# Five filling matmuls of 512 columns become 45 of 32 columns in a hash-attention and MLP kernel on one core

## The chip, the core and the metric

The kernel runs on one core of a Trainium2 chip. A core has five engines with instruction streams of their own: TensorE (matrix multiply; its records are PE for matmuls and PEld for weight loads), VectorE (DVE), ScalarE (ACT), GpSimd (POOL) and SyncE (SP), which here only issues transfers. They work side by side and wait for each other by semaphores. Operands lie in an on-chip memory of 128 partitions (SBUF), matmuls write to accumulators (PSUM), and the DMA engines move data between these and the device's memory.

The metric is the device time of one execution in microseconds. Before the change it is 292.64 us, the median of three runs (292.36 to 292.85).

## What is computed

Attention over 4 batches, 8 heads, 768 positions and 64 dimensions, in which a query sees only the keys of its own bucket; a bucket is given by the signs of six projections. Then a normalised two-layer MLP with a residual, on rows of 512 features.

```python
q_bits = (np.einsum('bhsd,dk->bhsk', q, proj) > 0).astype(np.int64)
k_bits = (np.einsum('bhsd,dk->bhsk', k, proj) > 0).astype(np.int64)
...
mask = q_bucket[:, :, :, None] == k_bucket[:, :, None, :]
scores = scale * np.matmul(q, k.transpose(0, 1, 3, 2))
scores = np.where(mask, scores, -1000000000.0)
...
return np.matmul(attn, v).astype(np.float32)
...
xn = (x - mu) / np.sqrt(var + 1e-06) * g_ln
ch = np.maximum(xn @ w_ch1, 0.0) @ w_ch2
return (x + ch).astype(np.float32)
```

## The kernel before

The work is cut into twelve units `u` of 256 query rows (three to a batch). Each unit runs through six score steps `s`, for two groups of four heads and three stretches of 256 keys, and then through the MLP.

- `S_` (matmuls of line 570) makes the scores of one step in three passes: one multiplies the sign bits `G`, which puts queries and keys of different buckets far apart, and two multiply q and k (`qb`, `kb`). Each pass runs as four matmuls on 32 rows of the array. `E_` (line 576) is the exponential on ScalarE. `A_` (line 595) multiplies its result with the values: 16 matmuls of 65 columns to a step, each with weights of its own, so 48 matmuls where three steps follow each other.
- `na`, `nb`, `nc_`, `ag` and `ce` (lines 608 to 630) normalise on VectorE. `F_` (line 659) and `P_` (line 726) are the two MLP layers on TensorE; the first unit's second layer is `D_` (line 674). `R_`, `Y_` and `ss` between them run on VectorE and ScalarE.
- The first batch's inputs are prepared on the fly at the start: `lx` loads q and k, `tn` transposes them on VectorE (line 304), `ca` casts them, `ha` or `hc` project them (lines 394 and 405), `sl` spreads the bits (line 418), `bh`, `bc` and `bi` turn them into `G`. `ft` (line 644) and `fc` (line 652) transpose the first unit's rows; the result is `xnT`.
- The weights of the MLP are loaded by eight transfers of 512 KB that GpSimd issues (`lw1`, `lw2`, lines 446 and 457) on the software queue q0; the other loads, the masks and the outputs go through the hardware queue q1, issued by SyncE.

No scheduler decides the order: the string `ORDER` lists every step as `name.engine.arguments`, each engine takes its own steps in that order, and semaphores are put in where one needs another's result. So TensorE's instructions form one fixed stream, and instructions are fetched from memory while the kernel runs, on DMA queues of their own that the profile calls "instruction".

TensorE's stream begins with fillers, matmuls of ones whose results nobody reads. `warm` issues eight of 512 columns while the first loads are under way. After it `wm` issues one more of 512 columns each time it stands in the order: `wm.t.0` and `wm.t.1` directly behind `warm`, `wm.t.2` and `wm.t.3` behind the first projections of step 0, ahead of its scores, and `wm.t.6` ahead of the scores of step 2:

```python
lg.s on.p.0 mem.v tab.a pf.v warm.t wm.t.0 wm.t.1 sel.p tn.v.0.0.0
p32.p tn.v.0.1.0 on.p.1 ca.a.0.0.0 pmem.p ha.t.0.0.0 bh.v.0.0.0 ha.t.0.1.0 bh.v.0.1.0 wm.t.2
wm.t.3 ca.a.0.1.0 tn.v.0.1.1 ca.p.0.1.1 tn.v.0.1.2 S.t.0.2 E.a.0.0 E.a.0.1 ha.t.0.1.1 bh.v.0.1.1
ha.t.0.1.2 bh.v.0.1.2 wm.t.6 ...
```

A weight load belongs to every matmul; in the profile each is a record of its own. `ones` is 128 x 128, and `row(4, P)` reads it four times, which gives the 512 columns.

Of the kernel before, what the change touches and what calls it, by code (L numbers as in the profile page):

```python
# [159 lines left out]
    x="012301320132",  # L160
# [5 lines left out]
def kernel(  # L166
# [15 lines left out]
    nc = tc.nc  # L182
    P = 128
# [35 lines left out]
    ones = pool.tile([P, P], BF16, name="ones")  # L219
# [9 lines left out]
    made, taken = {}, {}  # L229
# [127 lines left out]
    def row(n, m):  # L357
        return ones[:, :m].unsqueeze(1).to_broadcast([P, n, m])
# [4 lines left out]
            nc.tensor.matmul(wp[:, 0].rearrange("p (a x) -> p a x", x=P), ones, row(4, P), start=True, stop=True)  # L363

    def wm(eng, n):
        nc.tensor.matmul(
            made["warm"][:, 0].rearrange("p (a x) -> p a x", x=P), ones, row(4, P), start=True, stop=True,
        )

    def lx(eng, g, t, kp0, kp1):  # L370
        src = qk_view(t, 0, g).rearrange("p (c kp x) -> p c kp x", c=CC, kp=3)
# [364 lines left out]
    def O_(eng, u, *a):  # L736
# [11 lines left out]

    OPS = dict(
        mem=mem, pmem=pmem, tab=tab, lp=lp, sel=sel, pf=pf, p32=p32c, warm=warm, wm=wm, lx=lx, tn=tn, ca=ca, ha=ha, bh=bh, hc=hc, bc=bc, sl=sl, bi=bi, lg=lg, gt=gt, gc=gc,  # L750
        lw1=lw1, wg=wg, lw2=lw2, on=on, lv=lv, cv=cv, su=su, sp=sp, sq=sq, sc=scp, LX=LX, gx=gx, tu=tu, CA=CA, hm=hm, bt=bt, mw=mw, mr=mr,
        S=S_, E=E_, A=A_, wa=wa, na=na, nb=nb, nc=nc_, ag=ag, ce=ce, rs=rs, fl=fl, ft=ft, fc=fc, F=F_, R=R_, D=D_, Z=Z_, P=P_, Y=Y_, sw=sw, ss=ss, O=O_,
# [37 lines left out]
```

## Time and profile before

| | |
|---|---|
| time, median of three runs | 292.64 us |
| the profiled execution | 292.61 us, span of its instructions 290.9 us |
| TensorE's matmuls | 4645, weight loads 4647 |
| `wm` (line 366) | 5 matmuls, first start 4.3 us, last 9.9 us |
| `warm` (line 363) | 8 matmuls, 1.1 to 4.1 us |
| DMA, mean over the span | 117 GB/s, 34.10 MB |

The profile is of one execution. Times in it count from the start of the span. A timeline row gives the start, the duration, the engine, the line and the operation (output and inputs by the program's names, the shapes, and how many it stands for); in brackets stands the idle time of the engine ahead of it and what ended it. "issue" means that the profile shows nothing that the engine waited for. A row of a table by windows gives the window, its length, then for each engine the busy time and, as "x", the number of records in it, then TensorE's granted clock, the mean busy share of the DMA engines, and the GB/s moved. In the DMA view a row gives a queue, its packets, MB, and the time that they took as a share of 16 engines over the window; shares can add up to more than 100%, since an engine can have two packets under way.

### The profile page before, as it was taken

The numbers are of one execution on the slowest core, as the hardware profiler recorded it, in microseconds if no ns is written. First come the engines' busy times: TensorE is split into PE (matmuls) and PEld (weight loads), VectorE is DVE, ScalarE is ACT, GpSimd is POOL, SyncE is SP. The second block draws the span as 40 slices with busy tenths as digits, with TensorE's granted clock in tenths as the row PEclk, the third lists the DMA queues.
The fourth block names the chain that finished last, engine by engine and source line by source line (L and its number), as shares of the span: only waits on it lengthen the run. The fifth ranks groups of instructions, "written<-read, shape, count | busy, mean of one in ns | idle before, by whom it ended". The sixth has DMA issues, their size and how long they took to land.

```text
span 290.9 us, 10520 instructions
## 1 busy us (share of the span) xinstructions
PE 282.9 (97%) x4645; PEld 227.0 (78%) x4647; DVE 207.0 (71%) x478; ACT 206.7 (71%) x236; POOL 53.8 (18%) x88
## 2 busy tenths in 40 slices
PE   8998999999999999999999999999999999999994
PEld 4776777648788887888778878877888878898883
DVE  5758898896779795797667995876665655782653
ACT  4889998998966978784865996887794694515140
POOL 4560426232431005000300107210010010001000
PEclk9999999999999999999999999999999999999999
DMA  6999997646544591364430352220310301404022
GB/s 191 365 303 271 214 278 135 141 116 167 179 122 130 132 335 56 125 114 136 95 82 1 83 133 64 61 55 7 92 34 8 74 2 24 107 0 99 12 74 73
DMA packets 31055, 34.10 MB, mean 117 GB/s; under 512 B 15521, under 2 KB 27809, under 8 KB 31010
## 3 DMA queue, kind: packets, MB, share of 16 engines
q1 hardware_dynamic: 25938, 28.72, 35.3%
q0 software_dynamic: 4224, 4.19, 8.7%
q8 instruction: 36, 0.59, 0.9%
q10 hardware_dynamic: 848, 0.53, 0.7%
q14 instruction: 9, 0.07, 0.1%
HBM read 27.86 MB, written 6.88 MB: 119 GB/s over the span
## 4 chain that ended last, share of the span: by engine, by line
PE 95%; DVE 2%; ACT 1%; issue 1%; ACTq 0%; DVEq 0%
PE f L659 30%; PE sc L570 18%; PE X L726 13%; PE acc L595 13%; PE Yb L726 7%; PE Ya L726 3%; PE hp L526 3%; PE hf L394 3%; PE f L674 2%; PE warm L363 1%; ACT E L576 1%; DVE xnT L652 0%; PE hf L405 0%; PE vp L487 0%; PE Yc L726 0%
## 5 line engine op out<-in xcount | busy, mean ns | idle before, releaser
L576 ACT ACTIVATE E<-sc,bias_sb 128x1024 bf16<-128x1024 f32 x144 | 153.2, 1112 | 34.3 <-PE sc L570 31.1
L659 PE MATMUL f<-xnT,w_sb 128*128 128x256 bf16 x768 | 94.2, 273 | 0.2 <-DVE xnT L652 0.2
L659 PEld LDWEIGHTS <-w_sb 128*128 128x128 bf16 x768 | 71.5, 98 | 12.6 <-issue 5.0
L667 ACT ACTIVATE hb<-f 128x512 bf16<-128x512 f32 x67 | 39.7, 598 | 34.1 <-PE f L659 34.1
L570 PE MATMUL sc<-qb,kb 32*128 32x256 bf16 x1152 | 52.4, 267 | 0.0
L595 PE MATMUL acc<-vaug,E 128*128 128x65 bf16 x1152 | 43.9, 194 | 0.9 <-issue 0.9
L595 PEld LDWEIGHTS <-E 128*128 128x128 bf16 x1152 | 40.9, 98 | 5.0 <-issue 3.7
L570 PE MATMUL sc<-G 6*128 6x256 bf16 (+1 forms) x576 | 42.3, 273 | 0.9 <-ACT E L576 0.8
L726 PEld LDWEIGHTS <-hb 128*128 128x128 bf16 x352 | 33.4, 98 | 5.4 <-issue 1.3
L635 POOL TENSOR_SCALAR rs<-mv 128x2 f32<-128x2 f32 x12 | 3.3, 278 | 152.5 <-DVE mv L624 152.4
L570 PEld LDWEIGHTS <-kb 32*128 32x128 bf16 x1152 | 30.3, 93 | 1.5
L731 DVE TENSOR_TENSOR x<-X,x 128x256 f32<-128x256 f32 x44 | 18.4, 420 | 15.6 <-PE X L726 15.3
L570 PEld LDWEIGHTS <-G 6*128 6x128 bf16 (+1 forms) x576 | 15.8, 91 | 16.3 <-issue 13.5
L669 DVE TENSOR_SCALAR hb<-f 128x512 bf16<-128x512 f32 x29 | 19.8, 682 | 12.2 <-PE f L659 12.0
L726 PEld LDWEIGHTS <-S 128*128 128x128 bf16 x264 | 25.0, 98 | 4.5 <-issue 1.3
L304 DVE STREAM_TRANSPOSE T<-X 128x384 f32<-128x384 f32 (+2 forms) x52 | 26.1, 536 | 0.0
L608 DVE SCALAR_TENSOR_TENSOR y<-vsB,acc 128x520 f32<-128x520 f32 x24 | 16.6, 692 | 9.8 <-PE acc L595 9.5
L726 PE MATMUL Yb<-w_sb,S 128*128 128x256 bf16 x176 | 22.9, 273 | 0.0
L726 PE MATMUL X<-wt,hb 128*128 128x256 bf16 x168 | 21.8, 273 | 0.0
L621 DVE BATCH_NORM_STATS2 st<-x 128x6 f32<-128x256 f32 x48 | 17.4, 412 | 0.2
L617 DVE TENSOR_TENSOR x<-y,rc 128x512 f32<-128x512 f32 x24 | 16.6, 692 | 0.8
L731 DVE TENSOR_TENSOR x<-Yb,x 128x256 f32<-128x256 f32 x22 | 9.3, 421 | 9.7 <-PE Yb L726 9.5
(95 smaller groups left out, 266.4 us busy)
## 6 DMA issues: line engine op xcount, KB each, us to landing
out_dram<-x SPq DMA_DIRECT2D x45, 128.0 KB
X<-in_k_dram SPq DMA_DIRECT2D x7, 768.0 KB
vn<-in_v_dram SPq DMA_DIRECT2D x24, 192.0 KB
X<-in_q_dram SPq DMA_DIRECT2D x6, 768.0 KB
w_sb<-in_moe_w_ch_dram POOLq DMA_DIRECT2D x8, 512.0 KB, 11.7
vn<-in_v_dram SPq DMA_DIRECT2D x2, 768.0 KB
X<-in_q_dram SPq DMA_DIRECT2D x2, 512.0 KB
Bd<-B SPq DMA_DIRECT2D x6, 96.0 KB
```

The lines of the kernel that those rows point to most:

```text
L304: nc.vector.transpose(d[:, j], s[:, j, kj0 : kj0 + n])
L570: nc.tensor.matmul(sc(s, i // 2)[:, i % 2, 256 * kk : 256 * kk + 256], lh, rh, start=(rep == 0), stop=(rep == 2), skip_group_check=True,)
L576: nc.scalar.activation(E(s)[:, heads(h)], sc(s, h), AF.Exp, scale=EXP_SCALE, bias=bias_sb)
L595: nc.tensor.matmul(acc[:, qt, (D + 1) * i : (D + 1) * (i + 1)], E(s)[:, i, 256 * kk + P * qt : 256 * kk + P * qt + P], vaug(u // 3)[:, 4 * ...
L608: nc.vector.scalar_tensor_tensor(yt(u, g), vs, EPS_ROW, made[f"acc{u}{g}"][:, :, :A], op0=AOP.mult, op1=AOP.add,)
L617: nc.vector.tensor_tensor(xo, a[:, :, :, 0:D], rc.to_broadcast([P, 2, 4, D]), op=AOP.mult)
L621: nc.vector.bn_stats(stats(u)[:, qt, g], xt(u)[:, qt, 256 * g : 256 * g + 256])
L659: nc.tensor.matmul(f1[:, n].rearrange("p (t x) -> p t x", t=2), w1_sb[:, dt, P * nt : P * nt + P], xnT(u)[:, :, dt], start=(dt == 0), stop ...
L667: nc.scalar.activation(hb(u)[:, 2 * p : 2 * p + 2], f1, AF.Relu)
L669: eng.tensor_scalar_max(hb(u)[:, 2 * p : 2 * p + 2], f1, 0.0)
L726: nc.tensor.matmul(f2, lh[:, n], rh[:, n], start=(first and n == 0), stop=(n == 7), skip_group_check=True)
L731: nc.vector.tensor_tensor(x, made[f"{prod(u, k)}{u}"], x, op=AOP.add)
```

## The change

`wm` issues a number of matmuls in place of one: 6 for `wm.t.0` and `wm.t.1`, 11 for `wm.t.2`, `wm.t.3` and `wm.t.6`, 45 in all. Each multiplies `ones` by the first 32 columns of `ones` and writes to the first 32 columns of the same accumulator. Forty more matmuls and forty more weight loads stand in TensorE's stream ahead of the scores of step 2. The order string is the same, and so are the streams of the other engines and the waits.

```diff
     def wm(eng, n):
-        nc.tensor.matmul(
-            made["warm"][:, 0].rearrange("p (a x) -> p a x", x=P), ones, row(4, P), start=True, stop=True,
-        )
+        for _ in range(6 if n < 2 else 11):
+            nc.tensor.matmul(made["warm"][:, 0, :32], ones, ones[:, :32], start=True, stop=True)
```

## The prediction

> **What bounds the kernel now.** I read the page first, then TensorE's waits, then the stretches around the two breaks that they show, and last the DMA view cut into short windows.
>
> ```profile
> span 290.9 us, 10520 instructions
> PE 282.9 (97%) x4645; PEld 227.0 (78%) x4647; DVE 207.0 (71%) x478; ACT 206.7 (71%) x236; POOL 53.8 (18%) x88
> q8 instruction: 36, 0.59, 0.9%
> PE 95%; DVE 2%; ACT 1%; issue 1%; ACTq 0%; DVEq 0%
> ...
> PE acc L595 <- issue: 0.9, 2, 0.6
> ```
>
> TensorE sets the end: it is busy for 97% of the span and makes 95% of the chain that ended last. So the time is the sum of its work and of its breaks. The last row, from the view of its waits, counts two breaks at line 595 that are put down to "issue", that is, to nothing that the profile shows. The timeline shows both (start, duration, idle time before it in brackets):
>
> ```profile
> 23.97 1.43 PE L595 MATMUL acc<-vaug,E 128*128 128x65 bf16 x41
> 25.74 0.27 PEld L595 LDWEIGHTS <-E 128*128 128x128 bf16 x7 [0.48 <-issue]
> ...
> 41.91 0.29 PE L418 MATMUL hf<-Bc,spread 128*128 128x64 bf16 x4
> 42.03 1.26 PE L595 MATMUL acc<-vaug,E 128*128 128x65 bf16 x36
> 43.86 0.42 PEld L595 LDWEIGHTS <-E 128*128 128x128 bf16 x12 [0.68 <-issue]
> ```
>
> Each break cuts a run of 48 equal matmuls in two (41 + 7, 36 + 12), where no other engine is waited for. Together they cost 0.48 + 0.68 = 1.16 us. The distance between them says what they are:
>
> ```profile
> 25.73:43.85 18.12, 16.62 (x383) 13.11 (x383) 16.07 (x39) 16.94 (x22) 4.95 (x9) 1.00 1.10 243
> ```
>
> From one break to the other TensorE runs 383 matmuls and 383 weight loads, 766 records. Queue q8 of the page fetches instructions in 36 packets, 0.59 MB; TensorE's 4645 + 4647 = 9292 records make 258 a packet, so a packet is 16 KB and holds some 256 instructions. 766 is three packets: both breaks stand at the edge of a block of instructions. Counted from them, five successive old blocks start and end here (window, its length, then TensorE's busy time and counts):
>
> ```profile
> 19.91:25.73 5.82, 5.00 (x133) 3.81 (x131) 3.92 (x11) 5.75 (x7) 0.83 (x2) 1.00 1.09 321
> 25.73:33.09 7.36, 6.41 (x127) 5.32 (x128) 6.67 (x17) 6.91 (x9) 1.10 (x3) 1.00 1.07 192
> 33.09:38.67 5.58, 5.58 (x129) 4.34 (x130) 4.56 (x11) 5.33 (x8) 3.62 (x6) 1.00 1.07 278
> 38.67:43.85 5.18, 4.63 (x136) 3.44 (x136) 4.83 (x12) 4.70 (x7) 0.23 (x1) 1.00 1.15 276
> 43.85:49.91 6.06, 6.05 (x127) 4.93 (x128) 5.15 (x11) 4.99 (x7) 4.26 (x4) 1.00 0.72 126
> ```
>
> The packets of q8 lie between. The DMA view of 23.48 to 24.44, 32.79 to 33.84 and 41.39 to 42.39 us (a share of 6.2% is one of 16 engines busy for the whole window):
>
> ```profile
> q0 software_dynamic: 46, 0.05, 29.0%
> q8 instruction: 1, 0.02, 6.2%
> ...
> q0 software_dynamic: 21, 0.02, 11.8%
> q8 instruction: 1, 0.02, 6.2%
> ...
> q0 software_dynamic: 148, 0.15, 88.9%
> q8 instruction: 1, 0.02, 6.2%
> ```
>
> So the packet asked for around the edge at 19.91 starts 3.57 us later and lands at 24.44; TensorE goes on at 25.74, 1.30 us after that. The packet of the edge at 38.67 starts 2.72 us later, lands at 42.39, and TensorE goes on at 43.86, 1.47 us after. The packet of the edge at 33.09, where the software queue q0 is nearly idle, starts 0.30 us before the edge, and nothing stops. I read this so: passing an edge asks for one block, the next edge needs it, and the packet waits behind bulk traffic, above all the weight loads of q0. Under load a block has to last 2.72 + 1.00 + 1.47 = 5.2 to 3.57 + 0.96 + 1.30 = 5.8 us, or TensorE breaks; without load -0.30 + 1.05 + 1.47, some 2.2 us, do. A late break would show as idle time, and from 60 us on there is none (the largest group there, its last column):
>
> ```profile
> L659 PE MATMUL f<-xnT,w_sb 128*128 128x256 bf16 x704 | 86.0, 273 | 0.0
> ```
>
> **What the change does to the fillers.** It takes out five filling matmuls of 512 columns and puts in 2 x 6 + 3 x 11 = 45 of 32 columns, each with its weight load. No row shows a 32-column matmul; the nearest are these:
>
> ```profile
> 6.46 0.59 PE L366 MATMUL warm<-ones 128*128 128x512 bf16 x2
> 6.66 0.42 DVE L307 TENSOR_SCALAR G<-hf 128x256 bf16<-128x256 f32 x1 [0.38 <-PE hf L394]
> 7.14 0.29 PE L570 MATMUL sc<-G 32*128 32x256 bf16 x4
> 9.90 0.38 PE L366 MATMUL warm<-ones 128*128 128x512 bf16 x1
> 10.02 1.09 ACT L311 ACTIVATE kb<-tp 128x512 bf16<-128x512 f32 x1
> 16.79 1.14 PE L595 MATMUL acc<-vaug,E 128*128 128x65 bf16 x32
> ...
> L595 PE MATMUL acc<-vaug,E 128*128 128x65 bf16 x1152 | 43.9, 194 | 0.9 <-issue 0.9
> ```
>
> Two fillers take 0.59 where one takes 0.38, so 0.21 each in a row. The 32 matmuls of 65 columns take (1.14 - 0.19) / 31 = 0.03 each with their weights; 32 columns cannot cost more, and at the least nothing. Six cost at most 0.18 against 0.21, eleven at most 0.34 against 0.21: for all five between -1.1 and +0.3 us of TensorE's own time. None of it is on the path: the pair at 6.46 would become 22 matmuls, which end at 6.46 + 0.66 = 7.12, and the score matmuls at 7.14 wait for VectorE's bits of 6.66 + 0.42 = 7.08 anyway. The last group delays the next scores by at most 0.13, and ScalarE, which reads them, has its cast of 10.02 until 11.11. I take 0, with up to +0.3 if that cover fails.
>
> **What it does to the edges.** All that follows stands 40 matmuls and 40 weight loads, 80 records, deeper, so each edge cuts 80 records earlier in the work. The edge inside the run at 23.97 moves back by 40 of its 41 matmuls, to its very start. The edge after 36 matmuls of the run at 42.03 moves back by these 36 (72 records) and by the four of line 418 (8), to 41.91. In the old times the new blocks are:
>
> ```profile
> 18.54:23.98 5.43, 4.95 (x132) 3.60 (x131) 3.32 (x9) 4.66 (x6) 2.20 (x4) 1.00 1.12 312
> 23.98:30.51 6.54, 5.43 (x132) 4.54 (x131) 5.12 (x15) 6.08 (x8) 0.00 (x0) 1.00 1.18 252
> ...
> 36.83:41.90 5.07, 5.07 (x131) 3.49 (x128) 4.93 (x12) 5.05 (x6) 1.47 (x1) 1.00 1.13 307
> 41.90:48.70 6.80, 6.24 (x132) 4.99 (x129) 5.59 (x14) 5.24 (x8) 4.48 (x4) 1.00 0.93 161
> 48.70:53.69 4.99, 4.99 (x129) 3.94 (x130) 4.68 (x11) 4.81 (x6) 0.00 (x0) 1.00 0.88 167
> ```
>
> *The old breaks go.* The second is worth its 0.68: TensorE never waits again after it. The first is worth less, since others wait in its train:
>
> ```profile
> 26.17 0.70 DVE L608 SCALAR_TENSOR_TENSOR y<-vsB,acc 128x520 f32<-128x520 f32 x1 [1.18 <-PE acc L595]
> 27.11 5.13 ACT L576 ACTIVATE E<-sc,bias_sb 128x1024 bf16<-128x1024 f32 x5 [0.45 <-PE sc L570]
> 28.28 0.28 PE L570 MATMUL sc<-G 32*128 32x256 bf16 x2 [0.35 <-ACT E L576]
> 29.44 0.85 PE L644 MATMUL ft<-ident,xc 128*128 128x128 bf16 x8 [0.33 <-DVE xc L628]
> 31.30 0.38 PE L659 MATMUL f<-xnT,w_sb 128*128 128x256 bf16 x2 [0.18 <-DVE xnT L652]
> ```
>
> ScalarE stood idle for 0.45 before 27.11 for scores that the break had delayed, and VectorE for 1.18 before 26.17. Both chains, and the three waits of TensorE on them, move up by 0.45, not 0.48. Gain: 0.45 + 0.68 = 1.13 us.
>
> *New breaks.* A block against its need of 5.2 to 5.8 us: the one of 5.43 gives a break of 0 to 0.4 at 23.98; I take 0.2, the middle, since its traffic is neither row's. The one of 6.54 (6.1 without the old break) gives none. The one of 5.07 gives 0.1 to 0.7 at 41.90; I take 0.35, nearer to the row of the same weight loads (2.72). The one of 6.80 less 0.68 is 6.1: none. The one of 4.99 breaks only if its packet falls under load (0.2 to 0.8); I take 0, since the stretch from 43.85 to 49.91, with a DMA share of 0.72, must have nearly free time, and the edge lies near its end. Sum of new breaks 0.55.
>
> **The sum:** 292.61 (the profiled execution, 1.7 above its span of 290.9) - 1.13 + 0.55 + 0 = 292.03. That execution lies 0.03 below the median of 292.64, so 292.0. Below, 0.2% is about what a measurement can tell from no change: 0.6 us, and the forecast sits just at that line.
>
> **The rivals.**
>
> (A) No edge breaks any more. For it: both short blocks, 5.43 and 5.07, are longer than the old ones without their breaks (5.82 - 0.48 = 5.34 and 5.18 - 0.68 = 4.50). Against: the need was above 5.07 in both measured cases. 292.64 - 1.13 = 291.5.
>
> (B) The breaks move and add up to the same, 0.9 to 1.5 us, because the loads come in a fixed train and some edge always meets it: 292.6, from 292.4 to 293.0.
>
> (C) Slower: the packet for the edge at 41.90 doesn't wait about 3 us but until the weight load before it in q0 has ended, and that load is stretched by the activations' loads beside it. The window from 41.39 has q0 at 88.9% as the packet starts, so it came in no quiet moment, and it may have been let in by one load's end. The old edge at 38.67 met that end soon; the new one at 36.83 asks some 1.8 us earlier and gains nothing by it: start 41.4, landing 42.4, TensorE goes on at 43.8, where it wants to at 41.90 - 0.45 = 41.45. Break 2.3 us, time 292.64 - 1.13 + 2.3 = 293.8. It decides from a start at about 40.1 on (break 1.1, all gain spent). Against: the packet of 19.91 started inside a load (q0 at 29% beside other traffic).
>
> (D) The breaks are no fetches, and the change moves nothing: 292.6. For it: the issue label names no cause. Against: the three packets between the breaks, and the landing shortly before each restart. [...] The trace speaks for two blocks held at a time.
>
> **How the numbers follow.** Forecast 0.38, A 0.18, B 0.14, C 0.24, D 0.06. Faster by over 0.2%: A and 0.24 of the forecast's 0.38, together 0.42. Within: the forecast's other 0.14, 0.08 of B, D's 0.06, 0.28. Slower: C and 0.06 of B, 0.30. The range reaches from a little below A, 291.3, to C with 293.8, and takes in the fillers' +0.3; alone the forecast's own range is 291.5 to 292.6.
>
> **What would show it.** In the changed profile the idle times at 25.7 and 43.9 us are gone; TensorE's waits put any break at about 24.0, 30.1, 41.5 or 48 us, 80 records before the old places, each 1.3 to 1.5 us after a q8 packet has landed; between breaks lie multiples of 256 records; after 60 us there are none. A break of over 1.1 us at 41.5 makes C right. Wrong would be breaks in the old places of the work, breaks that follow no packet, a break at 30 or 53 us that I set at nothing, or TensorE's clock falling back in the first 15 us because the small fillers keep it less busy.

## The result and the profile after

The changed kernel takes 291.82 us, the median of 20 executions (291.32 to 292.57), against 292.85 us for the kernel before in as many measured beside them (291.69 to 293.82). The ratio is 0.997, with an interval from 0.9959 to 0.998: about 1 us, 0.2 to 0.4%, faster.

The profiled execution took 291.63 us. Its page:

```profile
span 289.9 us, 10600 instructions
PE 283.2 (98%) x4685; PEld 228.1 (79%) x4687; DVE 207.5 (72%) x478; ACT 206.2 (71%) x236; POOL 53.5 (18%) x88
...
q8 instruction: 36, 0.59, 0.9%
...
L594 PE MATMUL acc<-vaug,E 128*128 128x65 bf16 x1152 | 43.5, 194 | 0.0
```

TensorE does the same work and 40 matmuls more, and the idle time at the line that was 595 (now 594; all lines behind `wm` have one number less) went from 0.9 to 0.0. The full list of TensorE's waits has no "issue" left:

```profile
PE warm L363 <- DVE bias_sb L320: 1.1, 1, 1.1
PE sc L569 <- ACT E L575: 0.8, 3, 0.4
PE ft L643 <- DVE xc L627: 0.2, 1, 0.2
```

In the timeline both runs of 48 matmuls, cut into 41 + 7 and 36 + 12 before, stand whole:

```profile
24.16 1.64 PE L594 MATMUL acc<-vaug,E 128*128 128x65 bf16 x48
25.64 0.28 PE L417 MATMUL hf<-Bc,spread 128*128 128x64 bf16 x4
...
41.56 0.29 PE L417 MATMUL hf<-Bc,spread 128*128 128x64 bf16 x4
41.69 1.63 PE L594 MATMUL acc<-vaug,E 128*128 128x65 bf16 x48
43.16 1.04 PE L658 MATMUL f<-xnT,w_sb 128*128 128x256 bf16 x8
```

The edges are where they were expected. The blocks between them, by windows (window, length, TensorE's busy time and counts first):

```profile
18.74:24.17 5.43, 4.95 (x132) 3.59 (x132) 3.32 (x9) 4.65 (x6) 1.88 (x4) 1.00 1.10 302
24.17:30.27 6.10, 5.45 (x130) 4.53 (x130) 5.20 (x16) 5.99 (x8) 0.00 (x0) 1.00 1.18 247
...
36.48:41.56 5.08, 5.08 (x131) 3.49 (x128) 4.94 (x12) 5.06 (x6) 1.47 (x1) 1.00 1.11 305
41.56:47.62 6.06, 6.06 (x131) 4.94 (x128) 5.83 (x12) 5.09 (x8) 3.48 (x3) 1.00 1.04 183
```

What differs is the packets. The one for the edge at 24.17 starts at 21.27 and lands at 22.38; its DMA view over just that window shows it among the weight loads:

```profile
q0 software_dynamic: 188, 0.19, 103.8%
q8 instruction: 1, 0.02, 6.2%
```

It started 2.53 us after its edge at 18.74, where the prediction had 2.72 to 3.57. The one for the edge at 41.56 runs from 38.51 to 39.39, 2.03 us after the edge at 36.48. So they landed 1.79 and 2.17 us ahead of the crossings, and nothing stopped.

**Where the time is.** The first 48-matmul run starts at 23.97 us before and at 24.16 after. From there to the end of the span pass 290.9 - 23.97 = 266.9 us before and 289.9 - 24.16 = 265.7 us after, 1.2 less; that is about the two breaks of 0.48 and 0.68. The start took 0.2 back. Whether this 0.2 is the fillers' doing is taken up below.

### The profile page after: what moved, and what is told of

Same layout as the page of the kernel before. It is cut to its first block, busy times and chain, and to the rows that moved or that the text cites. A ratio compares the mean times of both kernels' runs of the same rounds, so it can differ in the third digit from the quotient of the medians.

```text
span 289.9 us, 10600 instructions
## 1 busy us (share of the span) xinstructions
PE 283.2 (98%) x4685; PEld 228.1 (79%) x4687; DVE 207.5 (72%) x478; ACT 206.2 (71%) x236; POOL 53.5 (18%) x88
## 4 chain that ended last, share of the span: by engine, by line
PE 95%; DVE 2%; ACT 1%; issue 0%; ACTq 0%; DVEq 0%
PE f L658 30%; PE sc L569 18%; PE X L725 13%; PE acc L594 12%; PE Yb L725 7%; PE Ya L725 3%; PE hp L525 3%; PE hf L393 3%; PE f L673 2%; PE warm L363 1%; ACT E L575 1%; DVE xnT L651 0%; PE warm L367 0%; PE hf L404 0%; PE vp L486 0%; PE Yc L725 0%
## 5 line engine op out<-in xcount | busy, mean ns | idle before, releaser
L616 DVE TENSOR_TENSOR x<-y,rc 128x512 f32<-128x512 f32 x24 | 17.9, 747 | 0.8
```

The lines of the kernel that those rows point to most:

```text
L616: nc.vector.tensor_tensor(xo, a[:, :, :, 0:D], rc.to_broadcast([P, 2, 4, D]), op=AOP.mult)
```

## The experiments

Edits are to the kernel before, unless said otherwise. The table has one profiled execution of each. "Depth" is the number of matmuls, each with its weight load, that stand in the stream ahead of the work beyond those of the kernel before. "Run" is the start of the first run of 48 matmuls, "breaks" the idle time of the weight loads at block edges, "rest" is span minus run minus breaks. The ratio averages over the executions, so a few long ones move it though the median stays. Line numbers differ by a few between the kernels.

| kernel | median us | ratio to before (interval) | run | breaks | span | rest |
|---|---|---|---|---|---|---|
| before | | | 23.97 | 0.48 + 0.68 | 290.9 | 265.8 |
| before, again (e9) | one, 293.08 | | 24.77 | 0.16 + 0.69 | 291.4 | 265.8 |
| changed | 291.82 | 0.997 (0.9959 to 0.998) | 24.16 | none | 289.9 | 265.7 |
| changed, again (e8) | 291.73 | 0.9966 (0.9947 to 0.9985) | 25.18 | see text | 292.7 | 267.5 |
| depth 40, in `warm` (e1) | 291.96 | 0.9978 (0.9962 to 0.9993) | 25.08 | none | 290.7 | 265.6 |
| depth 0, short (e2) | 292.44 | 1.0026 (0.9992 to 1.0059) | 23.92 | 0.36 | 290.0 | 265.7 |
| depth 128 (e3) | 293.47 | 1.0043 (1.0014 to 1.0072) | 24.59 | 0.61 and a small one | 293.5 | 268.3 |
| loads later (e4) | 293.17 | 1.003 (1.0011 to 1.0048) | 24.65 | none | 290.3 | 265.7 |
| loads later, again (e10) | 292.9 | 1.0014 (0.9997 to 1.0031) | 23.76 | 0.70 | 290.2 | 265.7 |

The medians of the kernel before beside them are 292.85 us (changed), 292.57 (e1 to e4), 292.64 (e5 to e8) and 292.63 (e9 to e12). The rest is 265.6 to 265.8 us in all profiles of the table but two, those of e3 and e8; in these TensorE's clock fell to half for a while, as told further down. Otherwise the start and the breaks account for the differences between the spans.

**The depth alone: 40 matmuls elsewhere (e1).**

```diff
-        for _ in range(NWARM):
+        for _ in range(5):
             nc.tensor.matmul(wp[:, 0].rearrange("p (a x) -> p a x", x=P), ones, row(4, P), start=True, stop=True)
+        for _ in range(43):
+            nc.tensor.matmul(wp[:, 0, :32], ones, ones[:, :32], start=True, stop=True)
```

> The five later fillers are as before (512 columns each); the 40 additional matmuls stand in the first group instead, where three of its eight 512-column fillers become 43 of 32 columns. Theory (only the place in the stream counts: 40 matmuls deeper, each block edge cuts 80 records earlier in the work): no break at lines 595, as in the changed kernel, and 1.0 to 1.3 us faster than before, 0.1 to 0.3 faster than the changed kernel, whose short fillers held up the first scores by 0.2 to 0.3. Rival (the short fillers near the first scores themselves bring the gain, by other timing there): both breaks of 0.48 and 0.68 us stay, time as before within 0.3 us.

Faster by 0.07 to 0.38%, and both runs whole, with the five later fillers untouched:

```profile
25.08 1.64 PE L597 MATMUL acc<-vaug,E 128*128 128x65 bf16 x48
...
42.61 1.63 PE L597 MATMUL acc<-vaug,E 128*128 128x65 bf16 x48
```

So the breaks went with the depth. The median is 0.6 us under that of before, less than the 1.0 to 1.3 expected, and the expected 0.1 to 0.3 us under the changed kernel did not come.

**The shorter fillers alone: depth 0 (e2).** Each of the five later fillers is a single matmul of 32 columns, so the stream keeps its length.

```diff
-        nc.tensor.matmul(
-            made["warm"][:, 0].rearrange("p (a x) -> p a x", x=P), ones, row(4, P), start=True, stop=True,
-        )
+        for _ in range(1):
+            nc.tensor.matmul(made["warm"][:, 0, :32], ones, ones[:, :32], start=True, stop=True)
```

> The five later fillers are one matmul of 32 columns each, so the stream has as many instructions as before. Theory (place in the stream): the breaks stay where they were, after 41 and after 36 matmuls of the two runs, 0.3 to 0.9 us each; time within 0.4 us of before. Rival (shorter fillers bring the gain): no break, about 1 us faster. Should the clock need these fillers, TensorE's granted clock falls in the first 15 us and the time is over 1 us longer.

```profile
23.92 1.64 PE L594 MATMUL acc<-vaug,E 128*128 128x65 bf16 x48
...
41.46 1.26 PE L594 MATMUL acc<-vaug,E 128*128 128x65 bf16 x36
42.96 0.42 PEld L594 LDWEIGHTS <-E 128*128 128x128 bf16 x12 [0.36 <-issue]
```

The second break is in its old place; the first is missing, which the theory had not foretold. No gain is measured. Single executions of this kernel ran from 291.7 to 296.0 us, wider than those of before in that group (291.6 to 293.84). The profiled one is the shortest. The four of 295.4 us and more have a mean granted clock of 0.993 or 0.994, the other eight 0.997 or more, so the long ones lost time at a lower clock; where in the kernel isn't on record.

**A whole block deeper: 128 matmuls (e3).** All 13 fillers become 141 of 32 columns: `warm` issues 106, `wm` 7 each time.

> All 13 fillers become 141 of 32 columns: 128 matmuls and 128 weight loads more than before, which is one block of 256 instructions, so that the edges cut the work in the same places as before. Theory (blocks of 256): the breaks are back after 41 and after 36 matmuls of the two runs, 0.2 to 1 us each, and the time is not under that of before minus 0.3 us. Rival (more and shorter fillers help as such, or any deeper stream does): no break, 1 us faster, as the changed kernel. The start may be held up by some tenths of a us if short matmuls run slower at the clock of the first 4 us.

The edges cut the work in the old places again, and the break after 36 matmuls is back:

```profile
24.59 1.84 PE L594 MATMUL acc<-vaug,E 128*128 128x65 bf16 x48
...
43.59 1.26 PE L594 MATMUL acc<-vaug,E 128*128 128x65 bf16 x36
45.34 0.42 PEld L594 LDWEIGHTS <-E 128*128 128x128 bf16 x12 [0.61 <-issue]
```

The first run takes 1.84 us for 1.64, so some 0.2 is lost at its edge too. So neither many short fillers nor any deeper stream helps; the depth counts within a block of 256 records. The slower time is not the breaks' alone: this profile shows TensorE's clock at half rate for 3.4 us, and five of the ten executions have a mean clock of 0.994 or less. The other five took 292.3 to 292.8 us, about as before.

**The same stream, other traffic: three weight loads later (e4, e10).**

```diff
-lw1.p.2 ... lw2.p.3 ... lw2.p.1 ... A.t.9.2 CA.p.1.0.1 na.v.1.1
+... A.t.9.2 CA.p.1.0.1 lw1.p.2 lw2.p.3 lw2.p.1 na.v.1.1
```

> The kernel before with its fillers and its stream position untouched; three of the eight weight loads (512 KB each) are issued some 6 us later, behind the cast of k that ends at 38.5 us. Theory (the second break is an instruction packet that waits behind this traffic): the packet that started at 41.4 us starts by 39.5 us, the break after 36 matmuls is gone or under 0.2 us, the one after 41 matmuls stays at 0.4 to 0.6; time 0.4 to 0.8 us under before, if the later traffic makes no new break at 48 to 58 us. Rival (the break belongs to the place in the stream or to the run of small matmuls, not to the traffic): it stays at 0.5 to 0.9 us and the time stays within 0.3 us.

```profile
42.18 1.63 PE L595 MATMUL acc<-vaug,E 128*128 128x65 bf16 x48
```

The DMA view of 39.68 to 41.24 us has its packet:

```profile
q0 software_dynamic: 74, 0.08, 53.0%
q8 instruction: 1, 0.02, 6.2%
```

With the stream as before, the second break is gone: the packet now runs from 39.68 to 41.24, 0.87 us after its edge at 38.82 (2.72 before), and TensorE crosses 2.02 us after the landing. The first break is missing here too, where 0.4 to 0.6 us were expected. The median is 0.6 us above that of before, and the ratio says slower, where 0.4 to 0.8 us under was expected.

> The kernel with three weight loads issued later, again: its profiled execution showed no break, yet the median lay 0.6 us above before. Theory: the packets of the edges at about 48 to 62 us now meet the later loads in some executions, so this profile, if it is one of the long ones (over 293.5), shows a break there, or TensorE's clock falling to half for 3.4 us as in two profiles of other kernels. If it shows neither, and the time is long, the waits for a weight load name another cause.

The second break is gone again, the first is there:

```profile
23.76 1.43 PE L595 MATMUL acc<-vaug,E 128*128 128x65 bf16 x41
25.77 0.27 PEld L595 LDWEIGHTS <-E 128*128 128x128 bf16 x7 [0.70 <-issue]
```

Both profiled executions are among the shortest of their groups (292.01 and 291.93), and both have an edge at 49.3 us crossed 1.24 and 1.32 us after its packet has landed, where the first profile of before has 2.20 us. The later loads now keep q0 busy up to that packet: over the window from 43 to 48 us its share is 105.2% in e4 and 91.1% before. That longer executions break there would fit, but no profile of one was taken: why this kernel is slower in the median stays open. It is no fall of the clock, since the mean clock of all 22 executions is 0.997 or more.

**The kernel before, again (e9).**

> The kernel before, for a second profile. Theory: a break wherever TensorE reaches an edge sooner than 1.3 to 1.5 us after the landing of that block's packet; the second break, after 36 matmuls, of 0.3 to 0.9 us, is there again, the first, after 41, may be anything from 0 to 0.6, since its margin was small. Rival (a fixed cost of these places): 0.48 and 0.68 again within 0.1.

```profile
26.23 0.27 PEld L595 LDWEIGHTS <-E 128*128 128x128 bf16 x7 [0.16 <-issue]
...
44.35 0.42 PEld L595 LDWEIGHTS <-E 128*128 128x128 bf16 x12 [0.69 <-issue]
```

The second break stands at 0.69 (0.68 before), the first at 0.16 (0.48 before). The first is no fixed cost: at the depth of before it was 0.48, 0.16, 0.70 and, in e2 and e4, nothing.

**Other depths: 72, 116 and 53 (e5, e6, e12).** For 72 and 116, `warm` issues 3 and 1 fillers of 512 columns and 77 and 123 of 32; `wm` is as before.

> Later fillers as before; in the first group five of eight 512-column fillers become 77 of 32 columns, so that all stands 72 matmuls (144 records) deeper. Theory (a break needs an edge that a block under the load of the first 50 us reaches before its packet): the edges fall where the block before them lasts long enough; no break, or one under 0.3 us; 0.6 to 1.3 us faster than before, as at a depth of 40. Rival (only the depth of 40 is good, or the edge must leave the runs of small matmuls): breaks of over 0.5 us in all.

This failed: 293.09 us, ratio 1.0015 (0.9993 to 1.0037), no gain. The profiled execution, 294.66 us, is one of five in twelve with a mean clock of 0.994 or less; the other seven have a median of 292.5 us, hardly a gain either. A break stands inside a group of score matmuls, so it needs no run of 65-column ones:

```profile
28.84 0.49 PE L572 MATMUL sc<-qb,kb 32*128 32x256 bf16 x8
29.78 0.29 PE L572 MATMUL sc<-G 32*128 32x256 bf16 x4 [0.45 <-issue]
```

Its packet had landed at 28.34, 1.44 us before. It had started 3.51 us after its edge, at the upper end of the old range.

> As the last, with 123 of 32 columns for seven of the eight: 116 matmuls deeper, which is 12 short of a whole block, so the edges cut the work 24 records later than before. Theory: the second edge falls behind all 48 matmuls of its run, ahead of the first layer's matmuls (line 659 before); the block before it ends sooner after its packet's request than before, so the break there is 0.6 to 1.4 us; the first break is 0 to 0.5; the time is that of before or up to 0.8 us over it. Rival (any deeper stream helps, or an edge breaks only inside the runs of 65-column matmuls): no break of over 0.2 us, faster than before.

293.36 us, ratio 1.0022 (1.0004 to 1.004): slower, as expected, but the break is smaller, 0.42 against 0.6 to 1.4. It stands behind the whole run:

```profile
41.84 1.63 PE L597 MATMUL acc<-vaug,E 128*128 128x65 bf16 x48
43.77 0.77 PEld L661 LDWEIGHTS <-w_sb 128*128 128x128 bf16 x8 [0.42 <-issue]
```

The matmul at 43.77 carries the note "ACT E"; its packet had landed 1.39 us before.

> As the last, with another 512-column filler of the first group given for 14 of 32 columns: 53 deeper, so that the edges cut the work 26 records earlier than at a depth of 40. Theory: the edge at 42 us moves back to about 41 us, the block before it keeps its length within 0.2 us, and no break is over 0.3 us; time within 0.3 us of the depth of 40. Against it speaks the depth of 72, where a break of 0.6 us came at 30 us: if the edge there is reached sooner after its packet already at 53, a break of 0.2 to 0.5 us stands at 30 us and the time is that much longer.

292.81 us, ratio 1.0016 (0.9982 to 1.005), no gain shown. At 30.3 us TensorE crossed 1.50 us after the landing without a clear break; at 41.88, 1.41 us after, the weight loads stood idle for 0.30 us, a small break. The expectation of a time within 0.3 us of the depth of 40 failed. Four of the twelve executions have a mean clock of 0.991 to 0.994 (293.8 to 295.4 us), and the other eight a median of 292.2; the profile, of 292.82 us, is none of the four.

**Shorter late fillers at a depth of 40 (e7, e11).** `warm` issues 7 of 512 and 14 of 32 columns, `wm` 7 for `wm.t.2` and `wm.t.3` and 6 otherwise.

> The changed kernel's depth of 40 with shorter late fillers: 6, 6, 7, 7 and 6 of 32 columns, and 14 of them for one 512-column filler of the first group. Theory: no break, as in the changed kernel, and the first scores start 0.1 to 0.3 us earlier than there at the same clock; time 0 to 0.3 us under the changed kernel's, 1.0 to 1.3 under before. Rival (the longer fillers are needed to hold the clock): the clock falls back in some runs, and the time is over that of the changed kernel.

291.56 us over five executions, ratio 0.9946 (0.9932 to 0.9961).

> Depth of 40 with the shorter late fillers, again, since only five executions stood behind its time: 0.8 to 1.6 us faster than before, a break of at most 0.2 us at the edge at 42 us.

291.72 us over twelve, ratio 0.9985 (0.9952 to 1.0018), since three of these took 293.8 to 295.0 us. These three have a mean clock of 0.991 to 0.994, the others 0.996 or more: the rival's sign, a clock that falls back in some runs, did come in the second group. Its profile, at 291.15 us, has no break. A gain over the changed kernel isn't shown.

**The changed kernel, again (e8).**

> The changed kernel, for a second profile and for times on the same chip as the other three. Theory: no break at line 594, packets land over 1.5 us before TensorE crosses the edges at about 24 and 41.5 us; 0.8 to 1.2 us faster than before. If the first profile's lack of breaks was luck, this one has a break of 0.2 us or more.

Its median, 291.73, repeats the result. Both runs are whole, though TensorE crossed the edge at 44.02 only 1.43 us after its packet's landing, where over 1.5 was expected. The profiled execution took 294.41 us, the longest of the twelve, and the windows say where (TensorE's granted clock is the third number from the end):

```profile
27.50:31.00 3.50, 2.85 (x56) 2.16 (x48) 3.26 (x11) 3.39 (x6) 0.00 (x0) 1.00 1.24 209
31.00:34.43 3.43, 3.43 (x37) 2.32 (x35) 3.43 (x9) 3.08 (x5) 1.52 (x3) 0.50 0.66 106
34.43:38.00 3.57, 3.57 (x88) 2.91 (x86) 1.21 (x4) 2.49 (x5) 1.73 (x4) 1.00 1.00 290
```

For 3.43 us the clock was at half. The work thus came later against the DMA traffic, and one edge, at 55.53, was crossed 1.58 us after its packet, behind a break of 0.48 us:

```profile
55.53 0.10 PEld L569 LDWEIGHTS <-kb 32*128 32x128 bf16 x4 [0.48 <-issue]
```

So the depth of 40 is not free of breaks in every execution.

## Why the prediction was right, and which size was off

- **Two breaks, blocks of 256, and the shift of 80 records.** Right. Both breaks went with the depth (e1), came back a block deeper (e3, the first at some 0.2 us), and stayed with other fillers at the old depth (the second, in e2). The new blocks came out at 5.43, 6.10, 5.08 and 6.06 us, where the prediction had 5.43, 6.1, 5.07 and 6.1.
- **A packet behind traffic.** Right for the second break: moving three loads let its packet start 1.71 us earlier (39.68 for 41.39) and took the break away, the stream untouched. For the first break the traffic was not varied, so there the cause is argued from its packet alone. In the twelve breaks named here, at edges from 25.7 to 55.5 us, TensorE went on 1.28 to 1.62 us after the landing; among the edges up to 67 us without one, none was crossed sooner than 1.24 us after it. That two blocks are held at a time is the author's estimate from these times: each start that is given here against an edge lies between 0.30 us before it and 3.57 us after it, and the packet was needed at the next edge. Rival D, no fetches at all, doesn't fit: both breaks moved with the depth (e1, e3), and the second went when only the loads moved (e4, e10).
- **Gain of 1.13 us.** About right: 1.2 between run and end. But the second profile of before has 0.16 + 0.69, so 0.45 for the first break is one draw of a term that went from 0 to 0.70.
- **New breaks of 0.55 us.** This is the term that was off: there were none. It used a wait of 2.72 to 3.57 us from the edge to the packet's start, taken from two edges. At the new ones it was 2.53 and 2.03; why it was shorter there isn't shown.
- **The time.** Inside the kernel, rival A happened, no break at all, to which the prediction gave 0.18. Against the 292.85 measured beside it the change is 1.03 us, close to A's 1.13 and not to the forecast's 0.6. That the forecast of 292.0 (292.06 by its own sum, taken from the median) lies so near the measured 291.82 is luck in part: the kernel before came out 0.21 us longer here than in the three runs that the prediction started from.
- **Fillers at nothing.** Borne out, by an estimate from six profiles. In the four with the fillers of before (before, e4, e9, e10) the trace records TensorE's full clock from 4.1, 5.8, 6.1 and 3.9 us on, and the run starts at 23.97, 24.65, 24.77 and 23.76 us: later by about 0.44 us for each us that the clock comes later. In the two of the changed kernel the clock is full from 5.1 and 7.1 us on, and the run starts at 24.16 and 25.18, some 0.1 us earlier than that line gives. By this the 0.2 us that the start took back are the clock's, not the fillers'.
- **C, the weight load's end.** Fell: the packet started at 38.51 while the load's queue q0 was still at work (29.5% from 38.51 to 39.39 us), 2.9 us before the 41.4 that C needed. B fell too, since no break came in another place.

## What to carry to other kernels

Where an engine is busy all the time and still breaks off with "issue" in the middle of equal instructions, count its instructions between the breaks: multiples of one packet of the instruction queue (here 766 records for three packets) suggest that a fetch came late, as the experiments with the depth and with the loads showed here. It can then be cured from two sides, by where the edges fall (fillers move them; the 40 more of the change cost the start nothing, by the estimate above) or by the bulk transfers ahead of the packet, but either can move other edges to their limits, as in e4 and e5, and of the depths tried here only 40 paid. Profile the kernel twice before taking the size of such a break as a cost, since the first one here came out between nothing and 0.70 us in five profiles at the depth of before.

## What the runs showed of the hardware

TensorE's clock comes up at a different time in each execution, from 3.9 to 7.1 us after the first instruction in the fourteen profiles, and this moves the start more than the fillers do. The projections behind the first fillers, with the same instructions, in the two profiles of the changed kernel, the first and then the second:

```profile
4.87 2.07 PE L393 MATMUL hf<-tp,pfull 128*128 128x256 f32 x8
7.45 0.29 PE L569 MATMUL sc<-G 32*128 32x256 bf16 x4
```

```profile
4.87 3.08 PE L393 MATMUL hf<-tp,pfull 128*128 128x256 f32 x8
8.47 0.29 PE L569 MATMUL sc<-G 32*128 32x256 bf16 x4
```

Eight matmuls take 2.07 or 3.08 us, and all that follows is 1.0 us later. What sets off a fall of the clock as in e8 isn't shown: TensorE was busy for 2.85 of 3.50 us in the stretch ahead of it, but also in the same stretch of the changed kernel's first profile (26.48 to 29.98 us), where none follows. Three of fourteen profiles show such a fall, with the granted clock at 0.50 for 3.41 us in e3 and e5 and 3.43 us in e8, all starting between 30 and 31.1 us; in e8 it costs at most 1.8 us, the rest of 267.5 against 265.7, of which the gap at 55.53 is a part.

How often it comes can be read from the mean granted clock that is on record for most executions: 0.993 or 0.994 in the three profiles with a fall, 0.996 or more in the others. A mean of 0.994 or less, always with a time of over 293.7 us, stands beside 2 of 91 executions of the kernel before, 1 of 32 of the changed one, and none of e1, e4, e6 and e10; but beside 4 of 12 in e2, 5 of 10 in e3, 5 of 12 in e5, 3 of 17 in e7 and e11, and 4 of 12 in e12. These executions lie 1.4 to 3.6 us above the median of the others of their kernel. So some changes to the fillers went with frequent falls, and part of what e2, e3, e5 and e12 lost goes with these and not with the breaks. It isn't their length alone: e6, where all but one of the first fillers are short, has none.
